# One attention stage in front of two feed-forward layers: GpSimd arithmetic moved away, an order written by a planner

## The chip, the cores and the metric

The kernel runs on one core of a Trainium2 chip. The metric is the device time of one execution in microseconds (us); the table below gives the median of three runs. The profile is that of one execution.

## What is computed

For 4 batches, 8 heads, 576 tokens and 64 values per head, attention over 32 memory slots per head, then two feed-forward layers over the 2304 tokens with 512 values each:

```
a = softmax over the tokens of phi              # phi: [4, 8, 576, 32]
k_m, v_m = a^T k, a^T v                         # per head: [32, 64]
attn = softmax over the 32 slots of (q k_m^T / 8)
x = attn v_m, heads side by side                # [2304, 512]
h = x w_in;  y = (h * sigmoid(h)) w_out         # 512 -> 2048 -> 512
out = ((y w_a) * (y w_b)) w_out2                # 512 -> 1536 -> 512
```

The weights of both layers are 64-bit floats in HBM; the rest is 32-bit.

## The kernel before, in words

Every 128x512 tile of weights is loaded as 64-bit words, turned into a 32-bit value t and then into two fp32r parts, hi and lo, so that three fast matmuls (hi hi, hi lo, lo hi) stand for one exact one. For the first tiles (`load_w`, L93, and `load_split`, L130) ScalarE scales the upper words, VectorE clips, shifts, masks and multiplies (L107 to L124), and the sum (L127) and lo = t - hi (L75, in `split`) go to VectorE or GpSimd as the caller names them. Later tiles go through `convert` (L157), whose accumulating DMAs on GpSimd's queue do the sum and the difference.

The attention stage works batch by batch. `weights(b)` takes phi on 96 partitions, finds the maximum over the tokens (L450, then a transpose L455 and L459), spreads it back with a matmul against ones (L465), subtracts (L472, mostly GpSimd) and takes exponentials (L475). `memory(b)` (L506) multiplies these with k, v and a column of ones, in six chunks of 96 tokens per head, 32 array columns per head; L513 to L521 divide by the sums, L526 transposes v_m, and its hi and lo parts are written to vbd_hi and vbd_lo. `turn_q` (L539) transposes q in 32x32 blocks on VectorE. `scores` (L556) multiplies the block-diagonal k_m (kbd, L548) with the turned q, slot by slot on the partitions, four fp32 matmuls for each half of the heads, and L558 turns the result back to tokens on VectorE. `softmax` (L571 to L583 and L75) takes maximum, subtraction, exponential, sum, product, transpose and the hi and lo parts at_hi and at_lo; subtraction and product go to GpSimd or VectorE as the caller names them.

The first layer does not multiply x by w_in: `vw_first` (L256) multiplies v_m by w_in for a batch (tile m), and `emit_h` (L288) multiplies that by at_hi and at_lo, so that the stage after the softmax is already feed-forward. A unit is half of the tokens of one batch in one slice of 512 hidden values: four tiles of h (6 matmuls each, Silu L298, hi L299, lo L300) and four tiles of y (`emit_y`, L312, up to 12 matmuls each), added up on VectorE (L318). The rest of the kernel runs units slice by slice (f = 0 to 3), then the second layer (L742 for w_a and w_b, L763 for w_out2).

What sets the order: each engine has one queue and works it in order. In the kernel before, the calls at the end of the attention part (from `load_phi(0)` on) are written out by hand, and the framework's own scheduler, with its own costs, may move instructions of an engine from there. Loads go through SP's queue (L98, L421, L427, L437, L440 and, for later tiles, L161) and wait there for a free buffer.

Of the kernel before, what the change touches and what calls it, by code (L numbers as in the profile page):

```python
# [20 lines left out]
def attn_moe_moe2_kernel(  # L21
# [35 lines left out]
    LATER = (nc.vector, nc.gpsimd, nc.gpsimd)  # L57
    SPLIT = (0, 3)
    SPLIT_W = (0,)
    SPLIT_Q = ()  # L60
    SUMS = (3,)
    WARM = (16, 2, 0)
# [7 lines left out]
    W = 512  # L70
# [6 lines left out]
    def copy(eng, out, in_):  # L77
        if eng is nc.scalar:
            nc.scalar.activation(out=out, in_=in_, func=AF.Copy)  # L79
        else:  # L80
            eng.tensor_copy(out, in_)
# [8 lines left out]

    n_w = [0]

    def load_w(src, engs):  # L93

        n = n_w[0]
        n_w[0] += 1
        st = p_w.tile([128, W], U64, tag="st", bufs=3, name=f"st{n}")
        nc.sync.dma_start(out=st if len(src.shape) == 2 else st.rearrange("p (a b) -> p a b", a=src.shape[1]), in_=src)  # L98
        word = st.bitcast(F32).rearrange("p (n t) -> p n t", t=2)
        low = st.bitcast(U32).rearrange("p (n t) -> p n t", t=2)[:, :, 0]  # L100
        e = p_w.tile([128, W], F32, tag="e", bufs=2, name=f"e_{n}")
        t = p_w.tile([128, W], F32, tag="t", bufs=2, name=f"t_{n}")
        ei, ti = e.bitcast(U32), t.bitcast(U32)


        nc.scalar.activation(out=e, in_=word[:, :, 1], func=AF.Copy, scale=2.0**-112)
        nc.vector.tensor_scalar(  # L107
            out=e, in0=e, scalar1=TOP, scalar2=-TOP, op0=ALU.min, op1=ALU.max
        )
        nc.vector.tensor_scalar(  # L110
            out=ti, in0=ei, scalar1=3, scalar2=None, op0=ALU.logical_shift_left
        )
        nc.vector.scalar_tensor_tensor(  # L113
            out=ti, in0=ei, scalar=0x80000000, in1=ti, op0=ALU.bitwise_and, op1=ALU.bitwise_or
        )

        nc.vector.tensor_scalar(
            out=ei, in0=ti, scalar1=0xFF800000, scalar2=None, op0=ALU.bitwise_and
        )
        if engs[0] is nc.gpsimd:  # L120
            nc.scalar.activation(out=word[:, :, 0], in_=low, func=AF.Copy, scale=2.0**-52)
            nc.gpsimd.tensor_tensor(out=e, in0=word[:, :, 0], in1=e, op=ALU.mult)
        else:
            nc.vector.scalar_tensor_tensor(  # L124
                out=e, in0=low, scalar=2.0**-52, in1=e, op0=ALU.mult, op1=ALU.mult
            )
        engs[1].tensor_tensor(out=t, in0=t, in1=e, op=ALU.add)  # L127
        return t

    def load_split(where, src, name, engs=None):  # L130
        pool, tag, bufs = ring[where]
        engs = engs or LATER
        w32 = load_w(src, engs)
        hi = pool.tile([128, W], F32R, tag=tag, bufs=bufs, name=name + "h")
        lo = pool.tile([128, W], F32R, tag=tag, bufs=bufs, name=name + "l")
        split(nc.scalar, engs[2], hi, lo, w32)
        return hi, lo
# [19 lines left out]
    def convert(where, src, name, put, soon):  # L157
# [3 lines left out]
        nc.sync.dma_start(out=st if len(src.shape) == 2 else st.rearrange("p (a b) -> p a b", a=src.shape[1]), in_=src)  # L161
# [12 lines left out]
        pin(nc.scalar.activation(out=e, in_=word[:, :, 1], func=AF.Copy, scale=2.0**-112))  # L174
        pin(nc.vector.tensor_scalar(out=e, in0=e, scalar1=TOP, scalar2=-TOP, op0=ALU.min, op1=ALU.max))
        pin(nc.vector.tensor_scalar(out=ti, in0=ei, scalar1=3, scalar2=None, op0=ALU.logical_shift_left))
        yield
        pin(nc.vector.scalar_tensor_tensor(
            out=ti, in0=ei, scalar=0x80000000, in1=ti, op0=ALU.bitwise_and, op1=ALU.bitwise_or
        ))  # L180
        pin(nc.vector.tensor_scalar(out=ei, in0=ti, scalar1=0xFF800000, scalar2=None, op0=ALU.bitwise_and))
        yield
        pin(nc.vector.scalar_tensor_tensor(out=e, in0=low, scalar=2.0**-52, in1=e, op0=ALU.mult, op1=ALU.mult))  # L183
        if soon:
            nc.gpsimd.tensor_tensor(out=t, in0=t, in1=e, op=ALU.add)
        else:
            nc.gpsimd.dma_start(out=t, in_=e, accum_op=ALU.add)  # L187
# [5 lines left out]
        pin(nc.scalar.activation(out=hi, in_=t, func=AF.Copy))  # L193
        yield
        if soon:
            nc.gpsimd.tensor_tensor(out=lo, in0=t, in1=hi.bitcast(F32), op=ALU.subtract)
        else:
            pin(nc.scalar.activation(out=lo, in_=hi.bitcast(F32), func=AF.Copy, scale=-1.0))
            nc.gpsimd.dma_start(out=lo, in_=t, accum_op=ALU.add)
# [17 lines left out]
    def load_wi(f, c, engs=None):  # L217
        if f == 0:

            r0, c0 = 256 * (c % 2), 256 * (c // 2)  # L220
            src = w_in[r0 : r0 + 256, c0 : c0 + 256].rearrange("(a p) n -> p a n", p=128)
        else:
            src = w_in[c * 128 : (c + 1) * 128, f * W : (f + 1) * W]
        if engs is None:
            start_load(where1(2 * f), src, f"wi{f}_{c}", lambda *hl: wi.update({(f, c): hl}), PLAN_POOL if f == 1 else PLAN1)
        else:
            wi[f, c] = load_split(where1(2 * f), src, f"wi{f}_{c}", engs)

    def load_wo(f, c, engs=None):
        r0 = f * W + c * 128  # L230
        src = w_out[r0 : r0 + 128, :]
        if engs is None:
            start_load(where1(2 * f + 1), src, f"wo{f}_{c}", lambda *hl: wo.update({(f, c): hl}), PLAN1)
        else:
            wo[f, c] = load_split(where1(2 * f + 1), src, f"wo{f}_{c}", engs)
# [9 lines left out]
    def vw_first(b, kc, halves=(0, 1)):  # L245

        hi, lo = m_tiles(0, b, kc)
        mp = mm_pool[0].tile([128, W], F32, tag=mm_pool[1], name="mp")
        for hf in halves:
            n = 0  # L250
            for a in range(2):
                o = 6 * kc + (2 + a if b % 2 == 0 else 5 * a)
                vh, vl = (w[b // 2][:, o : o + 2].rearrange("p a n -> p (a n)") for w in (vbd_hi, vbd_lo))
                wh, wl = (w[:, 256 * a : 256 * a + 256] for w in wi[0, 2 * hf + kc])
                for x, y in ((vh, wh), (vh, wl), (vl, wh)):
                    nc.tensor.matmul(mp[:, 256 * hf : 256 * hf + 256], x, y, start=(n == 0), stop=(n == 5))  # L256
                    n += 1
        ns = slice(256 * halves[0], 256 * halves[-1] + 256)
        split(nc.scalar, nc.vector, hi[:, ns], lo[:, ns], mp[:, ns])

    def vw_in(f, bs, pr):

        o = 3 * pr + 1
        vh, vl = (w[bs[0] // 2][:, o : o + 2].rearrange("p a n -> p (a n)") for w in (vbd_hi, vbd_lo))
        mp = mm_pool[0].tile([128, W], F32, tag=mm_pool[1], name="mp")
        wh, wl = wi[f, pr]
        for n, (a, c) in enumerate(((vh, wh), (vh, wl), (vl, wh))):
            nc.tensor.matmul(mp, a, c, start=(n == 0), stop=(n == 2))  # L268
        halves = slice(0, 64), slice(64, 128)
        for i, b in enumerate(bs):  # L270
            hi, lo = m_tiles(f, b, pr // 2)
            r = halves[(pr + i) % 2]
            split(nc.scalar, nc.vector, hi[r], lo[r], mp[halves[(pr + i + 1) % 2]])
# [5 lines left out]
    def emit_h(u, c):  # L279
        f, b, hf, _ = u  # L280
        hp = ff["h"].tile([128, HALF], F32, tag="hp", name="hp")
# [3 lines left out]
        for kc in range(2):  # L285
            mh, ml = m_t[f, b, kc]
            for a, x in ((mh, at_hi), (mh, at_lo), (ml, at_hi)):
                nc.tensor.matmul(hp, a[:, cs], x[b][:, kc, ts], start=(n == 0), stop=(n == 5))  # L288
                n += 1
        g32 = ff["t"].tile([128, HALF], F32, tag="g32", name="g32")  # L290
# [7 lines left out]
        nc.scalar.activation(out=g32, in_=hp, func=AF.Silu)  # L298
        nc.scalar.activation(out=gh, in_=g32, func=AF.Copy)  # L299
        nc.vector.tensor_tensor(out=gl, in0=g32, in1=gh.bitcast(F32), op=ALU.subtract)  # L300
        g_t[u, c] = gh, gl

    def emit_y(u, o):
        f, b, hf, cs = u
        yp = ff["y"].tile([128, HALF], F32, tag="yp", name="yp")
        os = slice(o * 128, o * 128 + 128)
        n = 0
        for c in cs:
            gh, gl = g_t[u, c]
            wh, wl = wo[f, c]  # L310
            for a, x in ((wh, gh), (wl, gh), (wh, gl)):
                nc.tensor.matmul(yp, a[:, os], x, start=(n == 0), stop=(n == 3 * len(cs) - 1))  # L312
                n += 1
        ys = y_t[b][:, o, hf * HALF : hf * HALF + HALF]
        if f == 0 and cs[0] == 0:
            nc.scalar.activation(out=ys, in_=yp, func=AF.Copy)
        else:
            nc.vector.tensor_tensor(out=ys, in0=yp, in1=ys, op=ALU.add)  # L318
# [58 lines left out]
    ps_sc = tc.alloc_tile_pool(name="ps_sc", bufs=2, space=PSUM)  # L377
    mm_pool[:] = ps_t, "t"

    P = 96  # L380
    JP = S // P
# [4 lines left out]
    ones = p_c.tile([128, P], F32, name="ones")  # L386
    warm = p_c.tile([128, 1], F32, name="warm")
    kbd = p_c.tile([128, 2, 2, 128], F32, name="kbd")
# [446 lines left out]
```

## Time and profile before

| | |
|---|---|
| median of 3 runs | 895.93 us (895.15 to 896.79) |
| the profiled execution | 895.07 us |
| its span, first to last instruction | 893.3 us |
| mean granted TensorE clock | 0.964 |
| TensorE busy | 847.2 us (95%) |
| VectorE busy | 536.1 us (60%) |
| ScalarE busy | 406.3 us (45%) |
| GpSimd busy | 162.5 us (18%) |

PE is TensorE, DVE is VectorE, ACT is ScalarE, POOL is GpSimd, SPq the queue that issues loads. A granted clock of 1 is 2.4 GHz, 0.5 is 1.2 GHz. Busy times of TensorE are those of pipelined matmuls, so two neighbours may overlap: the distance between starts is the better price of one. An fp32 matmul leaves two records, an fp32r one or a transpose leaves one. L and a number is a line of the kernel.

### The profile page before, as it was taken

To read this page: it belongs to the slowest core of one execution; us is meant where nothing else is said; L and a number is where in the kernel's file an instruction comes from. 1 tells how busy PE (TensorE), PEld (TensorE's weight loads), DVE (VectorE), ACT (ScalarE), POOL (GpSimd) and SP (SyncE) were. 2 spreads that over 40 slices of the span, in tenths; PEclk is the share of its full clock that TensorE was granted. 3 is DMA by queue.
4 is the path that set the end of the run, shared out by engine and by line. 5 is a ranking of instruction groups with operands and counts; after the bars stand their busy time and mean duration, and the time that the engine had idled before them with its cause. 6 is when DMAs were issued, how large, how long until landed. Compare 5 with 4: busy or idle time off the path is not lost.

```text
span 893.3 us, 14183 instructions
## 1 busy us (share of the span) xinstructions
PE 847.2 (95%) x5654; PEld 799.8 (90%) x5654; DVE 536.1 (60%) x980; ACT 406.3 (45%) x819; POOL 162.5 (18%) x160
## 2 busy tenths in 40 slices
PE   5458899999999999999999999999999999999998
PEld 4347889999999999999999999999999999999997
DVE  3699688887777677766755544636445552233313
ACT  2347666686566566555444332333333332122211
POOL 3454003422210111121222111111111110000000
PEclk7557999999999999999999999999999999999999
DMA  9998410265752554364764434424343321110012
GB/s 213 244 202 211 108 27 26 83 152 109 156 122 45 116 127 99 85 143 105 160 134 98 92 84 95 95 59 93 85 95 72 83 48 24 36 36 20 24 30 71
DMA packets 49939, 87.16 MB, mean 98 GB/s; under 512 B 4561, under 2 KB 26065, under 8 KB 49873
## 3 DMA queue, kind: packets, MB, share of 16 engines
q1 hardware_dynamic: 33456, 56.50, 24.3%
q0 software_dynamic: 16128, 29.37, 18.7%
q8 instruction: 44, 0.72, 0.3%
q10 hardware_dynamic: 288, 0.39, 0.2%
q14 instruction: 23, 0.18, 0.1%
HBM read 52.17 MB, written 4.72 MB: 64 GB/s over the span
## 4 chain that ended last, share of the span: by engine, by line
PE 80%; DMA 7%; DVE 6%; issue 3%; ACT 2%; SPq 1%; POOL 1%; POOLq 0%; DVEq 0%; ACTq 0%
PE ab L742 32%; PE yp L312 19%; PE op L763 17%; PE hp L288 9%; DMA st<-in_moe_w_in_dram 3%; DMA t_w<-e_w 1%; PE mp L268 1%; PE mp L256 1%; PE sc L556 1%; DMA kv<-in_v_dram 1%; DVE t L113 1%; DMA wo_1l<-t_wo 1%; SPq L427 1%; DVE qT L539 1%; SPq L98 0%
## 5 line engine op out<-in xcount | busy, mean ns | idle before, releaser
L747 DVE TENSOR_TENSOR asb<-ab,asb 128x384 f32<-128x384 f32 x72 | 40.1, 557 | 198.8 <-PE ab L742 196.0
L746 ACT ACTIVATE asb<-ab 128x384 f32<-128x384 f32 x72 | 35.4, 491 | 148.8 <-PE ab L742 148.8
L79 ACT ACTIVATE ph<-asb 128x384 fp32r<-128x384 f32 x72 | 37.6, 522 | 118.9 <-DVE asb L747 118.8
L298 ACT ACTIVATE g<-hp 128x288 f32<-128x288 f32 x128 | 52.3, 411 | 79.9 <-PE hp L288 71.7
L300 DVE TENSOR_TENSOR gl<-g,gh 128x288 fp32r<-128x288 f32 x128 | 62.2, 488 | 38.5 <-ACT gh L299 38.1
L187 POOL DMA_DIRECT2D t_w<-e_w x36 | 31.8, 884 | 145.8 <-DVE e_w L183 130.3
L318 DVE TENSOR_TENSOR y<-yp,y 128x288 f32<-128x288 f32 x104 | 47.3, 456 | 18.4 <-PE yp L312 17.9
L299 ACT ACTIVATE gh<-g 128x288 fp32r<-128x288 f32 x128 | 56.4, 444 | 3.6 <-PE yp L312 0.3
L75 DVE TENSOR_TENSOR pl<-asb,ph 128x384 fp32r<-128x384 f32 x72 | 39.9, 554 | 20.7 <-ACT ph L79 20.7
L79 ACT ACTIVATE yh<-y 128x768 fp32r<-128x768 f32 (+1 forms) x48 | 29.5, 676 | 25.9 <-PE ab L742 25.9
L312 PE MATMUL yp<-gh,wo_1l 128*128 128x288 f32 x128 | 37.8, 296 | 1.5 <-DMA wo_1l<-t_wo 1.5
L312 PE MATMUL yp<-gh,wo_0h 128*128 128x288 f32 x128 | 38.4, 300 | 0.1
L312 PE MATMUL yp<-gh,wo_2h 128*128 128x288 f32 x128 | 38.2, 299 | 0.0
L312 PE MATMUL yp<-gl,wo_3h 128*128 128x288 f32 x128 | 37.8, 297 | 0.0
L312 PE MATMUL yp<-gl,wo_2h 128*128 128x288 f32 x128 | 37.8, 295 | 0.0
L312 PE MATMUL yp<-gl,wo_0h 128*128 128x288 f32 x128 | 37.8, 295 | 0.0
L312 PE MATMUL yp<-gh,wo_2l 128*128 128x288 f32 x128 | 37.7, 295 | 0.0
L312 PE MATMUL yp<-gh,wo_3h 128*128 128x288 f32 x128 | 37.7, 295 | 0.0
L312 PE MATMUL yp<-gl,wo_1h 128*128 128x288 f32 x128 | 37.7, 296 | 0.0
L312 PE MATMUL yp<-gh,wo_1h 128*128 128x288 f32 x128 | 37.7, 294 | 0.0
L312 PE MATMUL yp<-gh,wo_0l 128*128 128x288 f32 x128 | 37.7, 294 | 0.0
L312 PE MATMUL yp<-gh,wo_3l 128*128 128x288 f32 x128 | 37.6, 294 | 0.0
(416 smaller groups left out, 2861.4 us busy)
## 6 DMA issues: line engine op xcount, KB each, us to landing
t_w<-e_w POOLq DMA_DIRECT2D x36, 256.0 KB, 4.9
st_wi<-in_moe_w_in_dram SPq DMA_DIRECT2D x12, 512.0 KB, 4.3
st_wo<-in_moe_w_out_dram SPq DMA_DIRECT2D x12, 512.0 KB, 3.7
st_w<-in_moe_w_a_dram SPq DMA_DIRECT2D x12, 512.0 KB, 3.9
st_w<-in_moe_w_b_dram SPq DMA_DIRECT2D x12, 512.0 KB, 4.0
st_w<-in_moe_w_out_dram SPq DMA_DIRECT2D x12, 512.0 KB, 3.8
kv<-in_k_dram SPq DMA_DIRECT2D x8, 576.0 KB, 11.7
kv<-in_v_dram SPq DMA_DIRECT2D x8, 576.0 KB, 14.3
```

The costliest lines, as they stand in the source:

```text
L75: eng_lo.tensor_tensor(out=lo, in0=src, in1=hi.bitcast(F32), op=ALU.subtract)
L79: nc.scalar.activation(out=out, in_=in_, func=AF.Copy)
L288: nc.tensor.matmul(hp, a[:, cs], x[b][:, kc, ts], start=(n == 0), stop=(n == 5))
L298: nc.scalar.activation(out=g32, in_=hp, func=AF.Silu)
L299: nc.scalar.activation(out=gh, in_=g32, func=AF.Copy)
L300: nc.vector.tensor_tensor(out=gl, in0=g32, in1=gh.bitcast(F32), op=ALU.subtract)
L312: nc.tensor.matmul(yp, a[:, os], x, start=(n == 0), stop=(n == 3 * len(cs) - 1))
L318: nc.vector.tensor_tensor(out=ys, in0=yp, in1=ys, op=ALU.add)
L742: nc.tensor.matmul(abp, a[:, ks], yy[:, kc], start=(n == 0), stop=(n == 11))
L746: nc.scalar.activation(out=asb, in_=ps[0], func=AF.Copy)
L747: nc.vector.tensor_tensor(out=asb, in0=ps[1], in1=asb, op=ALU.mult)
L763: ins = nc.tensor.matmul(o_t[x], a[:, cols], w, start=(c == 0 and n == 0), stop=(c == 3 and n == 2))
```

## The change

phi, k and v are laid on 128 partitions: two heads, each with its tokens on 64 partitions in nine chunks, instead of one head on 96 in six. The maximum over phi's chunks is four pairwise maxima on VectorE; its subtraction is on VectorE. `memory` then takes 36 matmuls of 64 rows for each half of the heads and each of the two operands, instead of 24 of 96 rows.

For batches 0 and 1 (`NEW`), q is turned by TensorE (nine 128x128 transposes for each half of the heads, copied by ScalarE), k_m is turned as well, and the scores are made token by token: 72 matmuls of 64 rows, 32 output partitions and 32 columns each. Maximum and subtraction then read PSUM. Batches 2 and 3 keep the turn on VectorE.

Of the eight first weight tiles, five (one of w_in, all of w_out) get lo from TensorE, which sums ident t - hi + ident e in PSUM; ScalarE copies it. hi is made from t before the low part e is added. The other three stay on VectorE. The subtractions, products, sums and remainders that GpSimd did in this stage are on VectorE.

The order is made by a list scheduler in the program: every piece of work is a task that yields operations with an engine, a time, what they need and what buffers they take; `run` picks the operation that can start first, and among those of the same engine within 200 ns that of the lowest rank. What it emits is pinned (`keep_in_program_order`), so each engine's queue has this order. The feed-forward units have the last rank. The order of loads is a list written by hand. After the attention stage pinning ends, and the code from there on does the same operations as before.

```
+    V, A, GP, T, Y = (Pinned(e) for e in (nc.vector, nc.scalar, nc.gpsimd, nc.tensor, nc.sync))
...
+    def run(while_any):
+        while any(t[0] in while_any for t in tasks):
+            starts = [(start_of(t), t) for t in tasks]
+            starts = [(a, t) for a, t in starts if a is not None]
...
+            first, t = min(starts, key=lambda x: x[0])
+            eng = t[2][0]
+            rank, at, t = min(((t[0], a, t) for a, t in starts if t[2][0] == eng and a <= first + 200.0), key=lambda x: x[:2])
...
+            if eng == "D":
+                t[3] = end
+                end += 2000.0
...
     def memory(b):
+            yield op("T", 2200, [f"w{b}", f"kv{b}{hg}"], take=("bank", f"kvp{b}") if hg == 0 else None,
+                     free=[f"kv{b}{hg}"] + [f"ph{b}"] * hg)
...
-            for x in (0,) if b in SUMS else (1, 0):
+            for sums in (1, 0):
                 for c in range(JP):
                     for h in range(4):
+                        o = slice(32 * h, 32 * h + 32)
+                        x, r = (h // 2 + b) % 2, slice(64 * (h % 2), 64 * (h % 2) + 64)
+                        T.matmul(
+                            kvp[o, hg, 2 * D :] if sums else kvp[o, hg, : 2 * D],
+                            e[r, 2 * hg + x, c],
+                            ones[r, :1] if sums else kv[r, :, x, c * D : c * D + D],
                             start=(c == 0), stop=(c == JP - 1),
                         )
...
+    def turn(b, hg, n):
+        yield op("T", 700, [f"q{b}{hg}"] + [f"qT{b}{hg}"] * (n > 0), done=f"qT{b}{hg}" if n == 0 else None,
+                 take=[(BANK_Q[b], f"qt{b}{hg}{n}")] + [("qT", f"qT{b}{hg}")] * (n == 0))
...
+        for i in range(3):
+            T.transpose(qt[:, i], t["qq", hg][:, 128 * (3 * n + i) : 128 * (3 * n + i) + 128], ident)
+        yield op("A", 450, done=f"qt{b}{hg}{n}", free=[f"qt{b}{hg}{n}"] + [f"qq{b}{hg}"] * (n == 2))
+        A.activation(out=t["qT", hg][:, 3 * n : 3 * n + 3], in_=qt, func=AF.Copy)
 
     def scores(b, hg):
+        if b in NEW:
...
+            for jj in range(J // 2):
+                for par in range(2):
+                    for h in range(4):
+                        o, r = slice(32 * h, 32 * h + 32), slice(64 * par, 64 * par + 64)
+                        T.matmul(sc[o, par, 32 * jj : 32 * jj + 32], qT[r, jj, o], t["kT"][r, hg, o])
+
+            yield op("V", 750, take=("mxq", f"mxq{b}{hg}"))
...
+            V.tensor_reduce(out=mx, in_=scv, op=ALU.max, axis=AX.X)
...
+    def tile_of(what, c):
...
+        bank = kind, "ps" + name
+        yield op("T", 2000, [f"hi_{name}"], take=bank)
+        ps = bank_of(kind, "ps")
+        T.matmul(ps, ident, t, start=True, stop=False)
+        T.matmul(ps, minus, hi, start=False, stop=False)
+        T.matmul(ps, ident, e, start=False, stop=True)
+        yield op("A", 550, done=name, free=[bank[1], f"e_{name}", f"t_{name}"])
+        copy(A, lo, ps)
...
+    LOADS = (
+        "wi00 q00 phi00 kv00 wi01 kv01 wo00 wo01 phi10 q01 q10 kv11 kv10 wo02 wi02 phi20 wo03 wi03 q11 q20 kv20 kv21 kv30 phi30 q21 q30 q31 kv31"
+    ).split()
+    NEW = (0, 1)
+    RANK = (2, 5, 7, 8)
+    RANK_I = (6, 4, 2, 5)
+    RANK_O = (3, 5, 5, 6)
+    BANK_W = ("yp", "yp", "bank", "bank")
+    BANK_Q = ("yp", "bank")
+    BANK_I = ("yp", None, None, None)
+    BANK_O = ("hp", "bank", "bank", "bank")
     fill()
...
+    add(0, loads())
+    add(9, feed_forward())
...
+    run(range(9))
+    run((1, 9))
+    pinned[0] = False
```

The names in LOADS are a kind, a batch and a half of the heads (for weights: a tile). The planner books 1.7 us for a weight tile, 2.2 for a q, 2.0 for a phi and 3.8 for a k with its v. A softmax operation on 576 values is booked at 0.64 to 1.15 us, an h tile at 0.9 us on TensorE and a y tile at 0.42 us for each slice of 128 hidden values.

## Rows read from the trace of the kernel before

**Rows 1.** The page: busy tenths and granted clock in 40 slices of 22.3 us.

```profile
PE   5458899999999999999999999999999999999998
...
PEclk7557999999999999999999999999999999999999
```

**Rows 2.** Busy by stage: PE, PEld, DVE, ACT, POOL; clock, DMA share, GB/s.

```profile
0.00:84.60 84.60, 50.27 (x525) 39.70 (x526) 61.23 (x93) 35.28 (x72) 39.43 (x33) 0.62 0.98 217
84.60:160.00 75.40, 72.01 (x757) 68.50 (x756) 58.07 (x100) 52.44 (x110) 14.37 (x9) 1.00 0.23 62
160.00:200.00 40.00, 38.39 (x267) 36.65 (x267) 35.80 (x62) 30.90 (x69) 14.63 (x12) 1.00 0.51 129
200.00:893.30 693.30, 686.51 (x4112) 654.99 (x4110) 380.96 (x728) 287.66 (x570) 94.03 (x106) 1.00 0.39 85
```

**Rows 3.** TensorE's timeline to 84.6 us: start, us, then what.

```profile
25.18 2.79 PE L506 MATMUL kvp<-kv,ph 96*32 96x128 f32 x48 [3.62 <-DMA kv<-in_v_dram]
...
38.23 4.21 PE L556 MATMUL sc<-qT,kbd 128*128 128x288 f32 x8
...
48.35 4.21 PE L556 MATMUL sc<-qT,kbd 128*128 128x288 f32 x8 [1.55 <-DVE qT L539]
...
66.54 0.85 PE L288 MATMUL hp<-at_hi,m0h 128*128 128x288 f32 x2 [0.93 <-ACT at_hi L79]
...
84.59 0.30 PE L312 MATMUL yp<-gh,wo_0h 128*128 128x288 f32 x1
```

**Rows 4.** The chain that ended last, 48 to 78 us: start, us, then what.

```profile
48.22 2.15 DVE t L113
50.37 2.70 DVE mxa L450
...
78.05 3.63 PE sc L556 x8
```

**Rows 5.** VectorE's timeline at 23 us, with GpSimd idle.

```profile
22.99 0.69 DVE L113 SCALAR_TENSOR_TENSOR t<-e,t 128x512 uint32<-128x512 uint32 x1
```

**Rows 6.** Groups by line and form, 0 to 165 us: busy us, mean ns, idle before.

```profile
L113 DVE SCALAR_TENSOR_TENSOR t<-e,t 128x512 uint32<-128x512 uint32 x8 | 9.9, 1232 | 0.2
...
L539 DVE STREAM_TRANSPOSE qT<-qq 128x1152 f32<-128x1152 f32 x8 | 10.9, 1362 | 3.5 <-DMA qq<-in_q_dram 3.4
...
L298 ACT ACT_TABLE_LOAD x6 | 7.7, 1283 | 0.8 <-DVE gl L300 0.7
...
L583 DVE STREAM_TRANSPOSE xt<-x 128x576 f32<-128x576 f32 x4 | 3.1, 772 | 2.6 <-POOL x L578 2.6
...
L571 DVE TENSOR_REDUCE mxq<-x 128x18 f32<-128x576 f32 x4 | 3.0, 744 | 0.0
...
L575 DVE TENSOR_REDUCE smq<-x 128x18 f32<-128x576 f32 x4 | 2.9, 734 | 1.5 <-ACT x L573 1.5
```

**Rows 7.** The same chain elsewhere, TensorE at full clock: start, us, what.

```profile
81.69 0.80 PE hp L288 x6
...
92.28 1.93 PE kvp L506 x94
...
133.78 1.94 PE sc L556 x8
...
148.60 2.87 PE mp L256 x24
...
463.38 2.08 PE op L763 x9
```

**Rows 8.** TensorE's timeline: memory batches, sums, a pair of transposes.

```profile
17.12 2.77 PE L506 MATMUL kvp<-kv,ph 96*32 96x128 f32 x48
...
92.21 0.58 PE L506 MATMUL kvp<-ones,ph 96*32 96x1 f32 x48
...
130.37 0.38 PE L526 MATMUL vt<-ident,kvn 128*128 128x128 f32 x2
130.51 0.36 PE L256 MATMUL mp<-wi_0h,vbd_hi 128*128 128x256 f32 x1
```

More of the change, by code (lines that the diff above doesn't have):

```diff
@@ new lines, in attn_moe_moe2_kernel, with op @@
+    free_at = dict.fromkeys("DVAGT", 0.0)
+    made = {}
+    rings = dict(st=(3, []), e=(2, []), t=(2, []), ph=(2, []), kv=(2, []), qq=(2, []), qT=(2, []), x=(2, []),
+                 kvn=(1, []), mxq=(2, []), smq=(2, []), bank=(2, []), sc=(1, []), kT=(2, []), hp=(2, []), yp=(2, []), g=(8, []), m=(4, []), g32=(2, []))
+    tasks = []
+    def op(eng, ns, after=(), done=None, take=None, free=(), wait=100):
+        takes = [] if take is None else [take] if isinstance(take[0], str) else list(take)
+        return eng, ns, after, done, takes, free, wait
@@ new lines, in add, with start_of @@
+    def add(rank, gen, ready=0.0):
+        first = next(gen, None)
+        if first:
+            tasks.append([rank, gen, first, ready])
+    def start_of(t):
+        eng, _, after, _, takes, _, _ = t[2]
+        at = max(t[3], free_at[eng])
+        for x in after:
+            if x not in made:
+                return None
+            at = max(at, made[x])
+        for name, _ in takes:
+            bufs, keys = rings[name]
+            if len(keys) >= bufs:
+                x = "free", keys[-bufs]
+                if x not in made:
+                    return None
+                at = max(at, made[x])
+        return at
@@ new lines, in attn_moe_moe2_kernel @@
+    add(9, feed_forward())
+    for b in range(B):
+        add(RANK[b], weights(b))
+        add(RANK[b], memory(b))
+        add(RANK[b], values(b))
+        for hg in range(2):
+            for n in range(3 * (b in NEW)):
+                add(RANK[b], turn(b, hg, n))
+            add(RANK[b], scores(b, hg))
+        for kc in range(2):
+            if b == 0:
+                add(3, vw_first(0, kc, (0,)))
+                add(5, vw_first(0, kc, (1,)))
+            else:
+                add(RANK[b], vw_first(b, kc, (0, 1)))
@@ L671, in attn_moe_moe2_kernel @@
+    for c in range(4):
+        add(RANK_I[c], tile_of("wi", c))
+        add(RANK_O[c], tile_of("wo", c))
+    run(range(9))
+    run((1, 9))
+    pinned[0] = False
     for p in (ps_sc, ps_t, ff["h"], ff["y"], p_c, p_s, p_in):
```

695 lines of the change are left out of this document (361 added, 334 removed).

## Prediction

> **What bounds the kernel now.** I read the page's slices first: TensorE is busy 30% to 80% of each of the first four slices, 90% or more from the sixth on, and its granted clock is low only at the start [rows 1]. The table by stage says the same in microseconds: TensorE is idle 34.3 us of the first 84.6, then 3.4, 1.6 and 6.8 us in the three later stretches, all at full clock, while the first stretch has a mean clock of 0.62, a mix of the two levels 1.2 and 2.4 GHz [rows 2]. So from 84.6 us on the kernel is a TensorE queue that hardly stops; a change ahead of it is worth what it saves of TensorE time lost in that first stretch, less the TensorE work it adds.
>
> The timeline of TensorE shows why the stretch is so long. The memory sums of batch 0 get their last values from HBM at 25.18, its first scores start at 38.23, the second half's at 48.35, the first feed-forward matmul at 66.54, and the first matmul of the second layer only at 84.59 [rows 3]. The chain of waits from 48.22 to 78.05 is all VectorE (42 pieces, with some issue time between them; the first two and the TensorE piece that ends it are [rows 4]): batch 0's softmax queues behind weight tiles and the maximum of a later batch's phi. VectorE is also slowed while GpSimd works: a 128x512 scalar_tensor_tensor takes 0.69 us where GpSimd is idle [rows 5] and 1.23 us on average [rows 6].
>
> **The change, part by part.** Span and lost time are kept apart: span = TensorE's lasting work at 2.4 GHz + time lost to idling or the lower clock.
>
> *The bill before.* By 84.6 us TensorE had done, at full-clock prices [rows 7]: 4 memory batches at 1.93 = 7.7; 4 score batches at 1.94 = 7.8; 36 matmuls of v by w_in at 2.87/24 = 0.12, 4.3; 18 of the first layer at 0.80/6 = 0.133, 2.4; transposes and broadcasts about 1.8 (estimate: three rounds of small matmuls). Together 24.0, so 60.6 us were lost.
>
> *When the feed-forward can start afterwards.* phi, k and v come as 128 partitions with runs of 1152 and 2304 bytes instead of 768 and 1536. Ahead of batch 0's last k and v stand 4.6 MB, as before, when they landed at 25.18 [rows 3] at a mean 217 GB/s [rows 2]. Lower bound 21 (a fifth faster, from the longer runs), upper bound 25.2 (no gain); I take 23, nearer to what the row shows. The Trainium skill, DMA: Bandwidth & Descriptors, section Specifications, asks for at least 512 B per transfer for line rate; by it both layouts are there already, the landing stays at 25.2 and the result is 2 us later than mine. No run here shows the new runs.
> From 23 on: the data matmuls of the second half at 1.2 GHz, 2.77 [rows 8] x 1.5 (nine chunks of 64 rows instead of six of 96) = 4.2, to 27.2; reciprocal, copy, transpose, copy about 2.5, to 29.7; scores 2 x 1.7, the second behind the first's subtraction, to 36; then maximum 0.74, subtraction, exponential, sum 0.73 with its small operations, product, transpose 0.77, copy, remainder, at about 0.75 each [rows 6], some 7 with hand-overs, to 43. Sharing VectorE with the first half's chain and with one low-ranked operation at a time adds 2.5; one pair of fp32 identity matmuls in front on TensorE adds 2.5. **Start at 48**, bounds 43 and 60 (the low end without the two additions, the high end with three weight tiles and a memory batch in front, below).
>
> *What TensorE has done by then:* two memory batches and half of one at 2.9 (1.93 x 1.5), 7.2; 18 transposes of q at 0.07 (a pair of transposes starts 0.14 us ahead of what follows [rows 8]), 1.3; two token-wise score batches at 1.7, 3.4; three weight tiles at 1.95, 5.9; 12 matmuls of v by w_in, 1.4; small ones 1.2. Together 20.4, lost 27.6: **33.0 saved**.
>
> *TensorE work added over the whole kernel.* Memory: 8 x 0.97 = 7.7. Weight tiles: five of the eight are summed on TensorE, each by two fp32 matmuls of 512 columns and one fp32r; four fp32 matmuls of 288 columns take 1.94, so 0.86 for 512, and an fp32r one 2.08/9 = 0.23 [rows 7]: 1.95 x 5 = 9.8. Turning q and k: 40 transposes, 2.8. Token-wise scores, 72 matmuls of 32 columns: 24 of one column take 0.58 [rows 8], 24 ns each, so 1.7 instead of 1.94; four batches give back 1.0. The bound above is no overlap of tiles, 72 x 0.054 = 3.9, or 7.8 more in all; below, the columns alone would give 1.0. I keep 1.7, the nearest row. **19.3 added.**
>
> *VectorE.* It gets the softmax's subtraction and product and all of the remainders, and loses the transposes of q (1.36 each [rows 6]) and of the scores for batches 0 and 1 and the stretching by GpSimd. With the times in the planner's tasks, which agree with the rows where there is one (0.75 against 0.74 for a maximum), its list is 15.4 us each for batches 0 and 1, 20.5 each for 2 and 3, 26 for the eight weight tiles, and some 24 of feed-forward and the next stage's tiles between: 122 us (estimate). Over 90% busy from 20 us on, VectorE has batch 3 ready near 145 us. TensorE has until then about 27.6 lost, some 55 of attention work (36 for all four batches before, plus the 19.3) and three batches of feed-forward at 4 x 4.8 = 19 each and 11 of v by w_in, so it is at 150: it covers VectorE by 5 us only, and that cover gone, every microsecond of VectorE counts.
>
> *ScalarE.* Exponentials now come per half of a batch between the units' Silu: the six table loads for Silu before 165 us, 1.28 each [rows 6], become about ten, each with one back. ScalarE was busy 52 of 75 us there [rows 2], so feed-forward matmuls hide them, except around the start. That, a clock that rises only some microseconds after the start (before, in the fourth slice [rows 1]), and in-order queues that wait for a transfer which the planner expected sooner (it books 70 us for loads that take 95 at 217 GB/s) I price together at **4.0 lost** (bounds 0 and 14: one table load; ten us as in the window before the old start).
>
> *Moved queues.* All loads are now one list on SP, with the weight tiles of batch 0 among them; q10, kv10 and kv11 wait for buffers of batch 0 and hold up what is behind them, wo02 and wi02 first. Those are needed by the third unit, some 10 us after the start, so I book nothing. GpSimd keeps the memsets and the accumulating DMAs; with no arithmetic ahead of them these start no later. From 200 us on nothing of weight changes.
>
> *Sum.* -33.0 + 19.3 + 4.0 = -9.7 on a span of 893.3, 883.6. The profiled execution took 895.07, 1.8 outside its span, so 885.4; the median of the runs is 0.9 above it, so **886**. About 0.2% is what a measurement of this kernel can tell from no change, 1.8 us.
>
> **Rivals.**
> *Slower: the added TensorE work stands in front of batch 0.* Queues run in their written order. Two weight tiles at 1.2 GHz take 3.9 each and a memory batch of batch 1 5.4; if these lie ahead of the second half's scores, the start is at 61 and the time 886 + 13 = 899. It decides from a start of about 58. For it: back to back, the memory matmuls of batch 0 still took 2.77 [rows 8], at the lower level; against: batch 0's rank is below theirs, and planner costs make the tiles wait.
> *A larger gain.* A busier TensorE gets 2.4 GHz from some 30 us on, and the start comes at 44: 4 less, the 4 of later loss shrink to 1, and overlapping row tiles save half of the 7.7 on memory: 886 - 11 = 875. For it: dense fp32 and fp32r matmuls before 48 us double with the five tiles; against: the low mean clock of [rows 2] although TensorE was busy 60% there.
> *No change.* The queues are fixed by a plan with loads a quarter faster than these rows. TensorE then waits for k and v of batches 1 and 2 with feed-forward work queued behind; 10 us more is 896. That the written order were not kept would land here too. Against: compute lags the plan as well, by the lower clock.
>
> **How the numbers follow.** Forecast 0.47, larger gain 0.27, no change 0.10, slower 0.16. The forecast's own range is 879 to 893, from start 44 to 52 and its unknown prices. For eight in ten I go to 869 (the larger gain with its start at 43 and memory without any growth) and to 899 (the slower rival). Faster 0.75 (forecast, larger gain, and a little of the no-change case), same 0.08, slower 0.17.
>
> **What will show it.** First feed-forward matmul near 48 and the second layer's soon after; TensorE's busy time up by about 15 to 20 us (36 new transposes, five tiles); VectorE's 128x512 scalar_tensor_tensor at 0.69 throughout; GpSimd almost empty before 150 us; the stretch from 200 us on as before. Wrong if the start is past 58, if token-wise scores take over 3 us at full clock, or if TensorE idles more than 10 us between the start and 160 us.

## The result, and the profile after

The changed kernel takes **902.58 us** (median, 901.98 to 904.3) where the kernel before, beside it on the same chip, takes 895.54: a ratio of **1.0088, 95% interval 1.0059 to 1.0118**. It is slower by 7 to 8 us where 10 us of gain were forecast, and it lies above the range's upper end. Its profiled execution took 902.41 us, its span 900.6.

The table by stage, with the columns of [rows 2]:

```profile
0.00:84.60 84.60, 59.23 (x1348) 49.00 (x1349) 51.51 (x106) 40.22 (x80) 4.21 (x12) 0.84 0.57 191
84.60:160.00 75.40, 67.38 (x946) 62.34 (x945) 50.36 (x105) 48.77 (x95) 1.27 (x1) 0.98 0.29 92
160.00:200.00 40.00, 37.78 (x267) 36.31 (x266) 35.70 (x60) 31.33 (x65) 13.79 (x11) 1.00 0.32 86
200.00:900.60 700.60, 694.52 (x4170) 663.00 (x4168) 387.69 (x740) 295.46 (x587) 95.33 (x108) 1.00 0.39 87
```

TensorE is idle 25.4 + 8.0 + 2.2 + 6.1 = 41.7 us instead of 46.1 and busy 858.9 instead of 847.2: 11.7 more less 4.4 is the 7.3 us by which the span grew. From 160 us on the two kernels lose alike. Between 84.6 and 160 the changed one idles 8.0 instead of 3.4, and up to 84.6 it leaves 1348 matmul records and 1349 of weight loads where the kernel before left 525 and 526.

TensorE's timeline, first around the first scores, then at the start of the feed-forward, then two pieces of added work, and the first tile of y:

```profile
22.34 3.42 PE L69 MATMUL kvp<-kv,ph 64*32 64x128 f32 x70
...
28.00 0.26 PE L69 MATMUL sc<-kT,qT 64*32 64x32 f32 x7 [0.30 <-ACT kT L69]
29.08 1.53 PE L69 MATMUL sc<-kT,qT 64*32 64x32 f32 x128 [0.83 <-issue]
35.01 0.33 PE L69 MATMUL sc<-kT,qT 64*32 64x32 f32 x9 [4.39 <-issue]
...
48.52 0.38 PE L69 MATMUL hp<-at_hi,m0h 128*128 128x288 f32 x1
...
56.64 2.17 PE L69 MATMUL kvp<-kv,ph 64*32 64x128 f32 x72
58.74 1.13 PE L69 MATMUL ps<-t_wo,ident 128*128 128x512 f32 x2
...
60.88 0.77 PE L69 MATMUL kvp<-ones,ph 64*32 64x1 f32 x72
...
63.63 0.40 PE L69 MATMUL yp<-gh,wo_0h 128*128 128x288 f32 x1
67.28 0.40 PE L69 MATMUL yp<-gh,wo_0l 128*128 128x288 f32 x1 [3.25 <-issue]
...
73.24 1.42 PE L69 MATMUL sc<-kT,qT 64*32 64x32 f32 x144
74.59 0.55 PE L69 MATMUL qt<-ident,qq 128*128 128x128 f32 x3
```

The first feed-forward matmul stands at 48.52, as forecast, 18 us sooner than in [rows 3]. But TensorE stops in the midst of a series of equal matmuls, for 0.83 and 4.39 us in the first scores and for 3.25 us after the first matmul of y; the trace names no engine and no transfer for it ("issue"). Two more such stops, 1.29 us at 20.38 and 0.34 at 39.88, make 10.1 us by 68. The kernel before has one such stop in this stretch, in front of memory sums, which [rows 3] does not show; no run here looks into it:

```profile
54.17 0.82 PE L506 MATMUL kvp<-ones,ph 96*32 96x1 f32 x48 [1.61 <-issue]
```

A stop can cost more than itself. Behind the one that ends at 67.28 the granted clock is 0.52 for 5.7 us, nearly the lower level, so 2.7 us more are lost there (5.70 x 0.48):

```profile
67.30:73.00 5.70, 5.70 (x26) 5.70 (x26) 0.95 (x3) 4.26 (x9) 0.00 (x0) 0.52 0.32 117
```

The stops come at equal distances. Two rows of the same table, each for the stretch from the end of one stop to the start of the next:

```profile
21.60:28.25 6.65, 5.21 (x127) 4.41 (x128) 2.28 (x7) 1.98 (x7) 0.00 (x0) 0.75 0.91 243
29.05:30.65 1.60, 1.53 (x128) 1.42 (x128) 1.55 (x6) 0.09 (x1) 0.00 (x0) 0.50 1.05 406
```

In each TensorE works off 128 matmul records (64 fp32 matmuls of the program) and as many weight loads (127 of one kind in the first row), 256 instructions, whether that takes 6.65 us or 1.60. The view of the transfers has one packet in the queue for instructions in the stop that begins at 30.62, and one in the stop of 3.25 us:

```profile
q8 instruction: 1, 0.02, 1.3%
...
q8 instruction: 1, 0.02, 2.3%
```

The page has 52 such packets of 0.85 MB, 16 KB each. So this is TensorE waiting for its next 256 instructions: a block of 128 small records is worked off in 1.6 us, and the next one is not there. Not every end of a block stops it: the scores at 73.24 run through whole, though by count a block ends among them, some 7 us after the one before. The Trainium skill, Runtime: NRT & Kernel Launch, section Instruction fetch mechanics, says that blocks hold 256 instructions and that crossing from one to the next is mostly hidden; the trace agrees on the count and not on the hiding, with stops up to 4.39 us.

ScalarE's table loads, from the groups by line and form up to 165 us, and the first of them on the chain of waits behind 69 us:

```profile
L69 ACT ACT_TABLE_LOAD x17 | 21.8, 1283 | 1.0 <-PEq L975 0.7
```

```profile
69.84 1.28 ACT L69
...
77.22 1.28 ACT L69
...
86.44 1.28 ACT L69
```

There were 12 by 165 us before; now there are 17, and 11 of them stand in the chain between 48 and 168 us, where the chain before had one, for 0.83 us (at 125.34). The last remainder of the attention stage, with which all of the softmax is done, ends VectorE's work on it at 168.33, where it ended at 160.80 before (start and us):

```profile
167.57 0.76 DVE L69 TENSOR_TENSOR at_lo<-xt,at_hi 128x576 fp32r<-128x576 f32 x1 [0.75 <-ACT at_hi L69]
```

### The profile page after: what moved, and what is told of

Read it like the earlier page. It is cut to its first block, busy times and chain, and to the rows that moved or that the text cites. A ratio compares the mean times of both kernels' runs of the same rounds, so it can differ in the third digit from the quotient of the medians.

```text
span 900.6 us, 16309 instructions
## 1 busy us (share of the span) xinstructions
PE 858.9 (95%) x6725; PEld 810.7 (90%) x6725; DVE 525.3 (58%) x1008; ACT 415.8 (46%) x825; POOL 114.6 (13%) x132
## 4 chain that ended last, share of the span: by engine, by line
PE 83%; ACT 6%; DVE 5%; issue 3%; DMA 2%; POOL 0%; SPq 0%; ACTq 0%; POOLq 0%; DVEq 0%
PE ab L69 33%; PE yp L69 18%; PE op L69 17%; PE hp L69 8%; PE kvp L69 3%; PE mp L69 2%; ACT L69 2%; DMA qq<-in_q_dram 1%; PE sc L69 1%; PE ps L69 1%; DVE smq L69 1%; DVE t_wo L69 1%; DMA wo_1l<-t_wo 1%; ACT g L69 1%; ACT ph L69 1%
## 5 line engine op out<-in xcount | busy, mean ns | idle before, releaser
L69 ACT ACTIVATE asb<-ab 128x384 f32<-128x384 f32 x72 | 35.4, 491 | 147.4 <-PE ab L69 147.4
L69 DVE TENSOR_TENSOR gl<-g,gh 128x288 fp32r<-128x288 f32 x128 | 60.0, 469 | 54.6 <-ACT gh L69 54.4
```

What stands on the lines that cost most here:

```text
L69: ins = f(*a, **k)
```

## The experiments

Eight theories came up: **A**, the fetch of instructions; **B**, an unseen transfer in its place; **C**, added TensorE work is paid in full; **D**, VectorE sets the pace; **F** and **G**, loads held up on SP cost time or hide; **H** and **I**, table loads cost time or hide. All edits are to the changed kernel (ratio 1.0088), and ratios are to the kernel before beside them; 1% is 8.9 us. The edits are of two kinds. Some change the list of tasks, so that the planner orders everything anew; others leave work out of tasks that the planner still books, so that every queue keeps its order. Only the second kind gives clean prices.

### No idle matmuls at the start

```
-    WARM = 16
+    WARM = 0
```

> The 16 idle matmuls at the start (64 TensorE instructions) are left out; they feed nothing. Theory A, TensorE stops because its next block of instructions has not been fetched: the stops are tied to the count of instructions, so each falls 64 instructions later in the work. The stop of 4.39 us that stands 9 records before the end of the first score batch leaves that batch and falls into the work behind it; the one among the sums of phi at 20.38 comes some 16 matmuls (32 records) later or falls between series. Theory B, the stops belong to the data (a transfer or a buffer that the profile does not name): each stays at the same matmul of the same series. Time: within 3 us of the changed kernel by both.

```profile
28.30 1.74 PE L69 MATMUL sc<-kT,qT 64*32 64x32 f32 x144
...
33.77 0.26 PE L69 MATMUL sc<-kT,qT 64*32 64x32 f32 x8 [1.11 <-DVE x L69]
34.63 1.29 PE L69 MATMUL sc<-kT,qT 64*32 64x32 f32 x128 [0.60 <-issue]
38.36 0.34 PE L69 MATMUL sc<-kT,qT 64*32 64x32 f32 x8 [2.44 <-issue]
```

Measured 898.63, ratio 1.0043 (1.0023 to 1.0064). TensorE's timeline shows the first batch of scores whole, and the second cut at its 8th and 136th record. Before, the first was cut at its 7th and 135th, the second at its 104th (39.88). Behind the cut at 135 stood 9 records of scores, 9 transposes, 6 matmuls of v by w_in and 104 of scores: 128. Moved by 32 records, the next cut but one falls on 144 + 9 + 6 + 8 = 167 = 135 + 32. A is right to the record, and B is out. That the time fell by 4 us neither theory had.

### The column sums: on VectorE, then left out in unmoved order

```
+    def sums_of(b):
+        yield op("V", 1750, [f"w{b}"], done=f"es{b}")
...
+            V.tensor_tensor(out=o, in0=x, in1=y, op=ALU.add)
...
+                T.matmul(kvp[o, hg, 2 * D :], t["es"][r, 2 * hg + x], ones[r, :1])
...
```

> The column sums of the exponentials are made by four VectorE additions a batch (about 1.7 us) and 4 one-column matmuls for each half of the heads instead of 36, which takes about 256 TensorE instructions out of every batch and some 0.7 us of TensorE time at full clock. Theory A (instruction fetch bounds small matmuls): at least one of the five stops before 68 us goes, the feed-forward starts 2 to 5 us sooner, and the time falls by 4 to 9 us, to 894 to 899. Theory C (only TensorE's added work counts): 4 times 0.7 less, 899 to 901. Theory D (VectorE is the bound of this stage): 4 times 1.7 more, 905 to 909.

Measured 896.18, ratio 1.0017 (0.9992 to 1.0041), 6.4 us less, although VectorE got four additions more in each batch. That is in A's range, and D is wrong by sign. It does not rule C out: the sums of a half take 0.65 us at full clock (60.88 to 61.53), so leaving 8 of 9 chunks out of eight halves is 4.6 us of TensorE's time, not the 2.8 that this expectation and the next count, and two ratios of this size differ clear of noise only by some 3.4 us. Since the plan moved too, the sums were then only left out:

```
-                for c in range(JP):
+                for c in range(1 if sums else JP):
...
-                            start=(c == 0), stop=(c == JP - 1),
+                            start=(c == 0), stop=(c == (0 if sums else JP - 1)),
```

> Of the column sums of the exponentials only the first of nine chunks is multiplied (the sums are wrong, so the output differs), 256 TensorE instructions less for each batch, no VectorE work put in, order of all queues as in the changed kernel. Theory C (TensorE's own time): 4 times 0.7, 2.8 less, 900. Theory A (instruction fetch): at least the stop of 1.29 us in these sums goes and one other shrinks, 5 to 9 less, 894 to 898.

```profile
0.00:84.60 84.60, 64.20 (x1134) 53.73 (x1135) 58.99 (x120) 46.80 (x93) 4.22 (x12) 0.84 0.56 191
```

Measured 889.88, ratio 0.9972 (0.9949 to 0.9994): 0.0116 less, 10.4 us (give or take 3.3), for matmuls that take 4.6 us of TensorE at full clock. C, with 4.6, is too low for them. The stops up to 90 us are 5.7 in all instead of 10.1. The row by stage is that of a queue that runs on: 214 matmul records fewer were left by 84.6 us, and TensorE was busy 5 us longer, with more of the later work. The last remainder ends at 156.89.

### The tiles' sums left out in unmoved order

```
-        T.matmul(ps, ident, t, start=True, stop=False)
-        T.matmul(ps, minus, hi, start=False, stop=False)
-        T.matmul(ps, ident, e, start=False, stop=True)
...
-        copy(A, lo, ps)
+        copy(A, lo, e)
```

> The three matmuls that make each of the five weight tiles' lo on TensorE are left out (lo is a copy of the low part e alone, so the output differs); the planner still books them, so the order of all queues is that of the changed kernel. Theory C (added TensorE work is paid in full): 10.7 less, 892. If it is half covered by waits for other engines: 897. Theory D (VectorE's chain sets the end of the stage, TensorE waits anyhow): at most 3 less, 900.

```profile
0.00:48.00 48.00, 26.77 (x652) 23.17 (x653) 26.44 (x55) 17.56 (x36) 4.22 (x12) 0.71 0.70 239
```

Measured 902.41, ratio 1.0104 (1.0062 to 1.0146): nothing, for 10.7 us of TensorE work. C is out for the tiles too: with the noise, a gain over 3.2 us is excluded. The row says part of why: the mean clock of the first 48 us is 0.71, with the tiles it was 0.79, and the stops for instructions up to 90 us stayed 10.2 in all (6.5 in the scores, 3.7 in the memory sums). So the tiles' long matmuls were done while TensorE would have waited anyhow, or what their absence saved was lost again to the lower clock; this run does not part the two.

### VectorE's work taken out in unmoved order

```
-        V.tensor_scalar(out=e, in0=e, scalar1=TOP, scalar2=-TOP, op0=ALU.min, op1=ALU.max)
...
-        V.scalar_tensor_tensor(
-            out=ti, in0=ei, scalar=0x80000000, in1=ti, op0=ALU.bitwise_and, op1=ALU.bitwise_or
-        )
...
-        V.tensor_scalar(out=ei, in0=ti, scalar1=0xFF800000, scalar2=None, op0=ALU.bitwise_and)
```

> Three VectorE operations of each of the eight first weight tiles are left out (the clip, the sign and the mask, 0.42 + 0.69 + 0.42 = 1.5 us a tile, 12.2 us in all; the weights of the first slice are other numbers), with the plan untouched. Theory D (VectorE's work is on the path, as the prediction said: every microsecond counts): 8 to 12 less, 890 to 895. If VectorE waits with the others for the hand-overs: 1 to 4 less, 898 to 901.

```profile
0.00:84.60 84.60, 60.99 (x1346) 50.00 (x1347) 40.76 (x84) 39.80 (x80) 4.21 (x12) 0.82 0.57 191
```

Measured 901.14, ratio 1.0083 (1.0052 to 1.0113): nothing again, with VectorE busy 40.76 instead of 51.51 us by 84.6. D is out for the tiles' arithmetic; VectorE's work in the softmax itself, which stands in the chain of waits, was not taken out.

### One table on ScalarE, alone and with few sums

```
...
-        A.activation(out=e, in_=e, func=AF.Exp)
+        A.activation(out=e, in_=e, func=AF.Silu)
...
-        A.activation(out=x, in_=x, func=AF.Exp, scale=scale)
+        A.activation(out=x, in_=x, func=AF.Silu, scale=scale)
```

> Exp is replaced by Silu in all three places, so the weights of both softmaxes are other numbers and ScalarE keeps one table: 17 of its 18 table loads before 185 us (1.283 us each) go, nothing else changes. Theory H (the table loads are on the path, as 11 of them stand in the chain between 48 and 166): 10 to 14 less, 888 to 893. Theory I (they hide beside TensorE's queue, as the prediction said): at most 3 less, 899 to 903.

> Column sums of one chunk only and Silu in place of Exp, both as in the runs before (both softmaxes are other numbers), plan untouched. Alone they gave 10.4 and 7.5 us by their ratios. If the costs are separate: a ratio of 1.0088 - 0.0116 - 0.0084 = 0.989, 885, as the prediction had it without either. If one hides in the other: 0.994 to 0.997.

```profile
0.00:84.60 84.60, 65.81 (x1223) 53.22 (x1227) 61.10 (x123) 42.17 (x92) 4.21 (x12) 0.92 0.57 191
84.60:160.00 75.40, 72.67 (x720) 69.29 (x712) 59.50 (x117) 41.86 (x102) 10.15 (x7) 1.00 0.35 112
```

```profile
144.97 0.76 DVE L69 TENSOR_TENSOR at_lo<-xt,at_hi 128x576 fp32r<-128x576 f32 x1 [1.84 <-ACT at_hi L69]
```

One table alone: 893.44, ratio 1.0004 (0.9979 to 1.0029), 0.0084 or 7.5 us less; the last remainder ends at 157.79. That is between H and I, nearer to H. Both together (the rows): 880.25, ratio **0.9853** (0.9814 to 0.9893), 21 us less, a little over the sum of the two. The last remainder ends at 145.73, and TensorE idles 2.7 us between 84.6 and 160. The same order of work, less 1024 small instructions (4.6 us of TensorE's time) and 17 table loads, comes out below the 886 that were forecast with both in it. But most of these sums and 12 of these loads stand in the kernel before as well, so not all of the 21 us is what the change added.

### Scores in half as many instructions

```
-                for par in range(2):
-                    for h in range(4):
-                        o, r = slice(32 * h, 32 * h + 32), slice(64 * par, 64 * par + 64)
-                        T.matmul(sc[o, par, 32 * jj : 32 * jj + 32], qT[r, jj, o], t["kT"][r, hg, o])
+                for h in range(4):
+                    o = slice(32 * h, 32 * h + 32)
+                    T.matmul(sc[o, 64 * jj : 64 * jj + 64], qT[:, jj, o], t["kT"][:, hg, h].rearrange("p r m -> p (r m)"))
...
```

> The changed kernel with k_m of batches 0 and 1 laid out block-diagonally, so that a half's token-wise scores are 36 matmuls of 128 rows and 64 columns instead of 72 of 64 rows and 32 columns: 144 TensorE instructions less for each of four half batches, no VectorE work more, one small ScalarE copy more for each batch. Theory A (instruction fetch): the stop of 4.39 us in the first score batch shrinks to under 2.5 or leaves that batch, one stop before 68 us goes, the last remainder of the attention stage comes 3 to 6 us sooner, 896 to 900. Theory C (TensorE work only): 4 times at most 0.6, 900 to 903.

Measured 899.3, ratio 1.0056 (1.0031 to 1.008): 2.9 us less, the stop of 4.39 us gone (0.6 us are left in all scores), but 2.1 us of stops in the memory sums. The first feed-forward matmul stands at 44.57, the last remainder ends at 164.31. The stop went as A has it; the time, at the weak end of A, is within noise of no change (3.4) and of C's 2.4.

### Old forms of scores and tiles

```
-        yield op("A", 1250, [f"sc{b - 1}0", f"sc{b - 1}1"] if b > 2 else [], done=f"kbd{b}")
+        yield op("A", 1250, [f"sc{b - 1}0", f"sc{b - 1}1"] if b > 0 else [], done=f"kbd{b}")
...
-    NEW = (0, 1)
+    NEW = ()
```

> Batches 0 and 1 get their scores as before the change: q turned by VectorE, four fp32 matmuls, result turned back by VectorE. About 270 TensorE instructions less for each of four half batches, TensorE time about equal (0.6 us more for each score batch, 0.7 less for its turns), VectorE some 2 us more for each. Theory A (instruction fetch): the stops of 4.39 us in the first score batch and 3.25 us in the first tile of y go or shrink to under 1 us, the feed-forward runs sooner, 893 to 899. Theory C (added TensorE work): no change, 901 to 904. Theory D (VectorE bound): 8 us more at most, 905 to 911.

```
-    BANK_I = ("yp", None, None, None)
-    BANK_O = ("hp", "bank", "bank", "bank")
+    BANK_I = (None, None, None, None)
+    BANK_O = (None, None, None, None)
```

> All eight weight tiles get their sum and lo on VectorE, none on TensorE: 5 times 2.14 = 10.7 us of TensorE work less, about 5 times 1.4 = 7 us of VectorE work more, 60 TensorE instructions less. Theory C (added TensorE work is paid in full): 10.7 less, 892. Theory D (VectorE bound): what TensorE saves it waits for VectorE, 899 to 906. Theory A by itself: no change from so few instructions, 900 to 903.

Measured 920.24 (1.0282) and 914.35 (1.0214), slower than all theories had it. TensorE's waits between 84.6 and 120 us with the old scores:

```profile
PE mp L69 <- ACT wi_3h L69: 11.2, 1, 11.2
PE kvp L69 <- ACT ph L69: 2.3, 1, 2.3
```

TensorE's head of queue stood 11.2 us for hi of the last w_in tile; in the changed kernel it never waited for that. With all tiles on VectorE it waited 4.9 us for the same. The planner had ordered all work anew. So these two runs price a plan along with a piece, and don't tell whether the piece itself was worth it. In that stretch of the first one VectorE was busy 17.87 of 35.4 us and TensorE 19.55, so neither was short of time, which speaks for the plan.

### The order of loads

```
-... phi20 wo03 wi03 q11 q20 kv20 kv21 kv30 phi30 q21 q30 q31 kv31
+... phi20 q11 wo03 wi03 q20 kv20 kv21 phi30 q21 kv30 q30 kv31 q31
```

> The list of loads alone is changed: q11 goes ahead of the last two weight tiles, phi30 and q21 ahead of kv30. In the changed kernel kv30 waits on SP from 64 to 100.5 for a k and v buffer, phi30, q21 and q30 stand behind it, and the chain then holds 10.6 us of waiting for a q at 101.95. Theory F (a load that waits holds up the loads behind it): that piece leaves the chain, the last remainder of the last softmax falls from 168 to about 160, the time falls by 4 to 9, to 894 to 899. Theory G (those loads hide behind the queue of feed-forward work and VectorE): within 2 us, 901 to 904.

The piece of the changed kernel's chain that F names:

```profile
101.95 10.62 DMA qq<-in_q_dram
```

Measured 908.3, ratio 1.0187 (1.0166 to 1.0208): 9 us more, which neither had. Here too TensorE waits 8.5 us for hi of the last w_in tile, so the plan moved. A smaller edit of the list, on top of two others, kept the order nearly as it was:

> Column sums on VectorE, no idle matmuls, and of the loads q21 alone moved ahead of kv30, which waits for its buffer until 93: the order of all other work stays nearly as it was, unlike in the earlier change of the load list. Theory F (the loads held up on SP cost time): q21 is issued before 80 instead of at 94 to 107, the third and fourth batches come 2 to 8 us sooner, a ratio of 0.994 to 1.000. Theory G (they hide): 1.0025, as without it.

```profile
66.34 0.34 SPq L69 DMA_DIRECT2D qq<-in_q_dram  x1
93.72 0.37 SPq L69 DMA_DIRECT2D kv<-in_k_dram  x1
```

SP's queue shows q21 issued at 66.34 and kv30 waiting to 93.72, and the ratio is 1.0061 (1.0041 to 1.0081) where 1.0025 stood without. F is out: that the chain of the changed kernel held 10.6 us of waiting for a q did not mean that an earlier q would be worth them. Why it got slower by 3 us is open.

### Together

> Column sums made by VectorE additions and no idle matmuls at the start, load list as in the changed kernel. If the two edits are separate: 902.6 - 6.4 - 4.0 = 892. If both only take instructions out of the way of the same stops: 895 to 897.

Ratio 1.0025 (1.0005 to 1.0044), 894.57: the second edit adds nothing to the first, as if both took instructions out of the way of the same stops. One of 1.84 us is left in the scores.

> Three edits together: column sums made by VectorE additions, the load list with q11, phi30 and q21 moved ahead, no idle matmuls at the start. The first took 6.4 us off the changed kernel and the third 4.0. If the fetch of instructions (A) and the held-up loads (F) are separate costs: 6.4 + 2 to 4 + 4 to 8 less, 884 to 891, faster than the kernel before. If they are one slack counted twice: 892 to 896.

Ratio 1.0194 (1.016 to 1.0229), outside both expectations: the moved plan again, with 9.0 us of waiting for the last w_in tile.

> Column sums on VectorE, no idle matmuls, and block-diagonal scores together. If stops for instructions are still on the path with the first two edits (a stop of 1.8 us is left among the scores): 1 to 4 less than those two alone, which stood 0.25% above the kernel before, so a ratio of 0.998 to 1.001. If they are used up: the same ratio, 1.0025.

Ratio 0.999 (0.9963 to 1.0017), 893.98, as for stops still on the path. No stop for instructions is left, and the first feed-forward matmul stands at 39.16.

> Column sums on VectorE, no idle matmuls, and a planner that knows which ScalarE table an operation needs: it books 1.283 us for a change of table and starts an operation without a change first where both could. If the table loads cost because the plan does not know them (H): fewer than 16 loads before 185 us, each plan time nearer to the chip's, 2 to 6 us less than without, a ratio of 0.996 to 1.001. If the later start of the postponed exponentials costs as much as the loads saved: 1.002 to 1.010.

Ratio 0.9989 (0.9962 to 1.0017), 892.23. The loads fell from 16 to 10, and the last remainder ends at 152.89. But TensorE's row has a new hole:

```profile
120.00:160.00 40.00, 32.29 (x326) 30.47 (x327) 29.54 (x61) 23.99 (x49) 3.36 (x3) 0.87 0.08 28
```

It idles 7.7 us while it waits for the postponed Silu and exponentials (one wait each of 3.7 and 4.1 us), and a stop of 4.05 us in the scores, 31.87 to 35.92, is still there.

> Column sums on VectorE, no idle matmuls, block-diagonal scores, and the planner that knows the tables. If fetch stops and table loads are separate costs, their gains add: the stop of 4.1 us left in the scores of the kernel with tables goes, a ratio of 0.994 to 0.998 to the kernel before, faster than both. If the end is set by work that both only wait for: 0.998 to 1.001.

> The same with the last tile of w_in loaded ahead of the last of w_out (the planner's order is otherwise the same): where TensorE waits 4 us for that tile's hi before the third unit, the tile comes about 2 us sooner. If that wait counts: 1 to 2 us less than without. If not: the same.

Ratios 0.9992 (0.9969 to 1.0015) and 1.0003 (0.9977 to 1.0029). The gains did not add, although neither trace has a stop for instructions: as in the run before, TensorE waits 3.7 and 4.1 us for the postponed Silu and exponentials in both. The earlier w_in tile gave nothing. With an attention stage that does all of its work, no version is clearly faster than the kernel before; four (0.999, 0.9989, 0.9992, 1.0003) are level with it, about a per cent faster than the change as it was made.

## Why the prediction was wrong, point by point

- **Start at 48: right in the number, by luck in the parts**, 48.52. The k and v came sooner than taken: the second half's v was issued at 4.54 and landed 10.8 us later, at 15.3, not at 23. The data matmuls of that half start at 22.34, behind the first half's at the lower clock (0.50 from 15.9 to 20) and a stop of 1.29. In the first 20.4 us the transfers moved 341 GB/s at a busy share of 0.95, where the kernel before moved 211 at 0.97, with about as many packets (3289 and 3227). So the longer runs went with a higher rate, though no run changes them alone. By the Trainium skill's rule (DMA: Bandwidth & Descriptors, Specifications) the landing would stay at 25.2; the trace disagrees. From 22.34 on, 5.6 us of stops (0.83, 4.39 and 0.34) stand about where the forecast had two allowances of 2.5 for other work. Without any stop, in the version with sums on VectorE, block scores and no idle matmuls, the start came at 39.16.
- **19.3 us of TensorE work added: right in size.** Memory 8 halves of 2.75 (55.99 to the tile at 58.74) instead of 1.93, 6.6; tiles 5 times 2.14 (58.74 to 60.88), 10.7; forty transposes at 0.1, 4.0; token-wise scores 1.35 (73.24 to 74.59), 0.6 less each, 2.4 for four. Together 18.9. **Wrong in what it costs**: the sum charged each of these microseconds. The 10.7 of the tiles cost nothing, and the column sums' 4.6 cost 10.4.
- **The step that failed: "4.0 lost" after the start** (bounds 0 and 14). TensorE's work by 48.5, at the prices above, is two memory halves 5.5, two score batches 2.7, 31 transposes 3.1, two tiles 4.3, 12 matmuls of v by w_in 1.4 and small ones 0.6: 17.6, so 30.9 were lost by then, against 27.6 forecast. The span before was 893.3 = 60.6 lost by 84.6 + 11.8 idle later [rows 2] + 820.9 of work. With 18.9 more work the span of 900.6 leaves 60.8 lost, 29.9 of them after 48.5: **18.1 more than before, not 4.0**, and beyond the upper bound. Of the 29.9 TensorE idled 23.9 (7.6 to 84.6, then 8.0, 2.2 and 6.1), and some 6 went to the lower clock, 2.7 of them behind the stop that ends at 67.28. Two things stand in its place. One, which the kernel before shows at most as a single stop of 1.61 us, is the fetch of instructions: the prediction priced matmuls by their time and never counted them, 525 to 1348 records by 84.6 us. Leaving out the column sums gave 10.4 us, 5.8 of them more than these matmuls' own time. The other, table loads, was named and set aside: "feed-forward matmuls hide them". They don't, 11 were on the chain, and 17 fewer gave 7.5 us; by five seventeenths, the five that the change added cost some 2.2 (estimate), and more if those of the kernel before mostly hid, as its chain suggests. These make 8.0 of the 14.1 missed. Block scores gave 2.9 more, which is not clear of noise. The rest stays open, as does how much of the stops before 48 is in both accounts.
- **"Over 90% busy ... every microsecond of VectorE counts": wrong.** VectorE was busy 82.2 of the 120.3 us between 48 and 168.33, 68%, and 12.2 us less of its work on the weight tiles gave nothing. By these runs what sets the pace is a chain that goes from engine to engine in a fixed order, and it lengthens where a hand-over does: a block of instructions, a table.
- **The rivals.** Slower at 899 was on the right side for another reason: no tile or memory batch stood in front of batch 0's scores. No change had loads behind a plan that is too quick; moving them did not help. The larger gain needs a start at 44: not reached.
- **What was to show it** came as written (start, busy time up by 11.7, the scalar_tensor_tensor at 0.65 to 0.69 in all 19 cases up to 165 us, GpSimd at 1.27 us between 84.6 and 160, from 200 us on as before), and yet the sum failed. Only "TensorE idles more than 10 us between the start and 160" named the loss: it idled 7.6 up to 84.6 and 8.0 behind.

## What to carry to other kernels

Count the instructions of a stage as well as their time: many matmuls of a few columns can cost more than the engine's busy time shows, and the sign is a gap without releaser in the midst of a uniform series, at equal counts. In a chain that crosses engines, take work out without moving the order before believing that an engine bounds it; here the weight tiles' work was worth nothing on TensorE or on VectorE, though TensorE was busy 29.03 of the 36.6 us between 48 and 84.6. Where a planner writes the order, an edit of one task prices a new plan as well: leave work out of booked tasks to price the piece.

## What was not expected of the hardware

- TensorE can stop at the end of 256 instructions where these are worked off fast: 128 small matmul records took 1.53 us, and the next block was 4.39 us late. The same boundary behind 6.65 us of work cost 0.83, and one behind some 7 us (by count, in the scores at 73.24) nothing. Such stops came beside busy transfers (the 4.39 at a share of 1.00) and idle ones (1.84 us at 0.07, with the sums on VectorE and no idle matmuls), so data transfers alone do not make them.
- Idle matmuls at the start, put there for the clock, cost time, whether by their instructions or otherwise: without them the ratio fell from 1.0088 to 1.0043, with a mean clock in the first 48 us of 0.82 instead of 0.79.
- Taking 10.7 us of long TensorE matmuls out of a stage with waits lowered the granted clock of the first 48 us from 0.79 to 0.71 and gave no time.
